# A 3072-point transform on one Trainium2 core: the sequence factored as 64 by 48 in place of 128 by 24

## The chip, the core and the metric

The kernel runs on one core of a Trainium2 chip. A core has TensorE (matrix products, into PSUM), VectorE, ScalarE and GpSimd (in the profile DVE, ACT and POOL), SyncE (SP), whose queue here only issues DMAs, and 16 DMA engines between HBM and SBUF. The metric is the device time of one execution in microseconds; the median of several runs counts.

## What is computed

Eight sequences of 3072 tokens by 256 features go through a spectral layer, then a soft mixture of experts, then a feed-forward layer. The reference, cut to the part that matters here:

```python
X = np.fft.rfft(x, axis=1)                  # x: 8 x 3072 x 256, float32
Xr, Xi = X.real, X.imag
Yr = Xr @ w_r - Xi @ w_i + b_r
Yi = Xr @ w_i + Xi @ w_r + b_i
Yr = np.sign(Yr) * np.maximum(np.abs(Yr) - lam, 0.0)   # lam = 0.01, Yi likewise
y = np.fft.irfft(Yr + 1j * Yi, n=3072, axis=1)
# then over all 24576 tokens of y: soft routing to 8 experts x 4 slots,
# and h = z @ w_in; out = (h * tanh(softplus(h))) @ w_out
```

The change concerns the first line alone, the forward transform, which is written as two stages of matrix products.

## The kernel before

A sequence of 3072 points is factored as 128 x 24: point 24 p + n has p on the 128 partitions and n with the 256 features along the row. **Stage 1** (`stage1`, product on line 193) multiplies by a 128 x 128 table of cosines and sines `f1` over p. A sequence has 6144 columns (24 x 256), taken 512 at a time (`XC`), so there are 12 products for each of 8 sequences, 96 in all, in float32. Each result is copied out of PSUM by ScalarE (line 197; for the first sequence every second one by VectorE, line 195) into a tile `a`. That tile is stored to the DRAM buffer `sdr` (line 200 for the first sequence, `store_a` on line 204 for the others), which turns the layout: `load_b` (line 210) reads it back as 96 rows for each of 32 positions `q`. A position holds two frequencies of the first stage, each with cosine and sine parts of 24 points, so 4 x 24 = 96 rows. **Stage 2** (`stage2`, line 222) multiplies each block of 96 rows by its own 96 x 144 table, a part of `tall`. ScalarE and VectorE split the result into a high and a low half (lines 230 and 231).

After that come, for each quarter `k` of a sequence (32 in all): `linear`, the three products with the weights in split float32 (tiles `l`, line 250), the threshold on VectorE, ScalarE and GpSimd, `project` (`pp`, line 281), `inv1` (`iu`, line 292) and `ytrans` (`tr`, line 307); and for each sequence the routing: `inv2`, the softmax steps, `fwd1` and `fwd2` (`dt`, line 434), `dturn` (`tn`, line 444) and `slots` (`sps`, line 457). `fwd1` and `inv2` use `f1` and its transpose `f1t` too. `pp`, `iu`, `dt` and `sps` and the products of the experts run in tiles of the array: the weights take 32 output columns, and three or four products stand side by side (`tile_position`).

The order is written by hand: every step is put on a list with a position, `at(pos, step, ...)`, the list is sorted, and each engine runs its instructions in that order. A unit of position is one quarter `k`. `s1pos(b, j)` gives the position of product j of sequence b: the loads, products and stores of sequence b + 2 or so run among the quarters of the sequences before. `load_x` and `store_a` handle two products (1024 columns) at a time. PSUM is one pool of 8 banks in rotation. The first sequence runs ahead of everything: twelve loads of x, twelve products, twelve stores, and 36 products that only keep TensorE running (`warm`). The feed-forward layer, the second half of the time, follows when all sequences are done.

Of the kernel before, what the change touches and what calls it, by code (L numbers as in the profile page):

```python
# [17 lines left out]

SEQ, D = 3072, 256
N1, N2 = 128, 24  # L20
NP = 32
NC = 384
NS = 32
# [5 lines left out]

def constants():  # L30

    n1 = np.arange(N1, dtype=np.float64)
    n2 = np.arange(N2, dtype=np.float64)
    f1 = np.zeros((N1, N1))
    t = np.zeros((96, NP, 96))
    w = 2.0 * np.pi / SEQ
    for i in range(64):
        p, par = divmod(i, 2)
        m, r0, c0 = 2 * i, par * 48, par * 24
        q = {0: 1, 1: 0}.get(i, i)  # L40
        if q:
            ang = 2.0 * np.pi * np.mod(n1 * q, N1) / N1
            f1[:, m], f1[:, m + 1] = np.cos(ang), -np.sin(ang)
            for k2 in range(N2):
                a = w * np.mod(n2 * (q + 128 * k2), SEQ)
                sg = 1.0 if k2 < 12 else -1.0
                t[r0:r0 + 24, p, c0 + k2] = np.cos(a)
                t[r0 + 24:r0 + 48, p, c0 + k2] = np.sin(a)
                t[r0:r0 + 24, p, 48 + c0 + k2] = -sg * np.sin(a)
                t[r0 + 24:r0 + 48, p, 48 + c0 + k2] = sg * np.cos(a)  # L50
        else:
            f1[:, m], f1[:, m + 1] = 1.0, np.where(n1 % 2 == 0, 1.0, -1.0)
            for pos in range(23):
                k, r = (128 * (pos + 1), r0) if pos < 11 else (64 + 128 * (pos - 11), r0 + 24)
                a = w * np.mod(n2 * k, SEQ)
                t[r:r + 24, p, c0 + pos] = np.cos(a)
                t[r:r + 24, p, 48 + c0 + pos] = -np.sin(a)
            t[r0:r0 + 24, p, c0 + 23] = 1.0
            t[r0:r0 + 24, p, 48 + c0 + 23] = np.where(n2 % 2 == 0, 1.0, -1.0)
    sel = np.tile(np.eye(NS), (4, 1))  # L60
    big = np.concatenate([f1, f1.T, np.eye(128), sel], axis=1)
    tt = t.transpose(2, 1, 0)
    t3 = np.concatenate([t, t[:, :, 0:48] + t[:, :, 48:96]], axis=2)
    both = np.concatenate([t3.reshape(96, -1), tt.reshape(96, -1)], axis=1)
    return np.ascontiguousarray(big.astype(np.float32)), np.ascontiguousarray(both.astype(np.float32))
# [3 lines left out]
def body(ctx, tc, x, w_r, w_i, b_r, b_i, phi, w1, w2, w_in, w_out, cbig, ct, out, dbg=None, stop=False):  # L69
    nc = tc.nc  # L70
# [31 lines left out]
    def psum(shape, name):  # L102
        return psp.tile(shape, F32, tag="p", name=name)
# [8 lines left out]
    m_run = [const.tile([128, 1], F32, name=f"m_run{i}") for i in range(2)]  # L112
    m_t, ab_t = {}, {}
    wsp = {n: (wp.tile([128, 2, D], F32R, name=n + "h"), wp.tile([128, 2, D], F32R, name=n + "l")) for n in "abc"}
    ph = wp.tile([128, 2, NS], F32, name="ph")
    bias = wp.tile([128, 2, 2], F32, name="bias")
    tlo = wp.tile([128, 2, 2], F32, name="tlo")
# [9 lines left out]

    def setup():
        nc.scalar.preload_act_table_set("natural_log_exp_and_others")
        nc.sync.dma_start(out=cb, in_=cbig)  # L130
        for j in range(na):
            load_x(0, j)
        load_t(0, 0)
        wst = ytp.tile([128, 6, D], F32, tag="yt", name="wst")
        wrf, wif = wst[:, 0:2], wst[:, 2:4]
# [32 lines left out]
        o = NP * 144 * i + g * w  # L168
        nc.sync.dma_start(out=tall[:, o:o + w], in_=ct[:, o:o + w])

    def load_x(b, j):

        w = XC if b == 0 else 2 * XC
        pool, tag = (xp, "x") if b else (yp, "y")
        t = pool.tile([128, w], F32, tag=tag, name="xc")
        src = x[b].rearrange("(p n) d -> p (n d)", p=128)
        nc.sync.dma_start(out=t, in_=src[:, j * w:(j + 1) * w])
        x_t[b, j] = t

    def stage1(b, j):  # L180
        if j == 0:
            sdr[b] = dram.tile([NP, 96, D], F32, tag="sdr", bufs=2, name="sdr")
        if b == 0:
            xs = x_t.pop((b, j))
            a = yp.tile([128, XC], F32, tag="y", name="a")
        else:
            c = slice(j % 2 * XC, j % 2 * XC + XC)
            xs = x_t[b, j // 2][:, c]
            if j % 2 == 0:
                a_t[b, j // 2] = xp.tile([128, 2 * XC], F32, tag="a", name="a")  # L190
            a = a_t[b, j // 2][:, c]
        ps = psum([128, XC], "s1")
        nc.tensor.matmul(ps, lhsT=f1, rhs=xs, start=True, stop=True)  # L193
        if b == 0 and j % 2:
            nc.vector.tensor_copy(a, ps)
        else:
            nc.scalar.activation(out=a, in_=ps, func=AF.Copy)
        if b == 0:
            dst = sdr[b].rearrange("q (r n) d -> (q r) (n d)", r=4)
            nc.sync.dma_start(out=dst[:, j * XC:(j + 1) * XC], in_=a)  # L200

    def store_a(b, i):
        dst = sdr[b].rearrange("q (r n) d -> (q r) (n d)", r=4)
        nc.sync.dma_start(out=dst[:, 2 * i * XC:2 * (i + 1) * XC], in_=a_t.pop((b, i)))
        x_t.pop((b, i))

    def load_b(k):
        b, g = divmod(k, 4)
# [674 lines left out]
```

## Time and profile before

| | |
|---|---|
| median of 3 runs | 1995.38 us (1994.22 to 2002.56) |
| the profiled execution, first to last instruction | 1995.2 us |
| TensorE busy | 1942.3 us, 97% |
| VectorE, ScalarE, GpSimd busy | 1169.1, 903.3 and 195.1 us |
| moved by DMA | 171.39 MB, mean 86 GB/s |
| granted TensorE clock, mean | 0.988 |

The profile is one execution. Its views are: the page, with busy time by engine, the chain of work that ended last, and the costliest groups of instructions; tables of busy time by stretch of time; instructions in order of time, where like ones that follow each other stand in one row with their count; and lists of what an engine waited for. Times are microseconds from the start of the span. TensorE works in a pipeline, so the duration of one matmul covers more than the time for which it keeps others out; the distance from start to start tells that.

### The profile page before, as it was taken

How to read it: one execution, taken by the hardware profiler on the slowest of the kernel's cores; microseconds unless marked ns; L12 is line 12 of the kernel's file. 1: busy time of each engine (PE TensorE's matmuls, PEld its weight loads, DVE VectorE, ACT ScalarE, POOL GpSimd, SP SyncE). 2: the span in 40 equal slices, each digit the busy share in tenths (PEclk: the TensorE clock that was granted, in tenths of full speed). 3: DMA queues.
4: the chain of work that ended last, by engine and by line, in shares of the span. 5: the costliest groups of instructions: out<-in, count | busy, mean ns of one | idle time of the engine just before them, and what ended most of it. 6: DMA issues, size and time to landing. Idle time of an engine off the chain costs nothing.

```text
span 1995.2 us, 30611 instructions
## 1 busy us (share of the span) xinstructions
PE 1942.3 (97%) x12344; PEld 1623.3 (81%) x12344; DVE 1169.1 (59%) x1767; ACT 903.3 (45%) x1479; POOL 195.1 (10%) x245
## 2 busy tenths in 40 slices
PE   7899999999998999999999999999999999999999
PEld 5677787777877768888888888888888888888887
DVE  3345545556455547666666666666666666666665
ACT  2666666667665433333333333333333333333332
POOL 0332332332323100000000000000000000000000
PEclk9999998999999899999999999999999999999999
DMA  8755665566643690002002002002002002000000
GB/s 248 233 151 173 167 185 141 170 173 160 184 142 78 213 297 27 20 13 53 22 22 53 22 22 53 22 22 53 11 22 53 22 22 53 22 22 22 22 22 22
DMA packets 131150, 171.39 MB, mean 86 GB/s; under 512 B 57136, under 2 KB 96688, under 8 KB 130752
## 3 DMA queue, kind: packets, MB, share of 16 engines
q1 hardware_dynamic: 128512, 164.10, 28.0%
q0 software_dynamic: 1792, 4.76, 0.8%
q8 instruction: 97, 1.59, 0.3%
q10 hardware_dynamic: 704, 0.57, 0.1%
q14 instruction: 45, 0.37, 0.1%
HBM read 102.29 MB, written 67.11 MB: 85 GB/s over the span
## 4 chain that ended last, share of the span: by engine, by line
PE 80%; ACT 9%; DVE 6%; issue 2%; POOL 1%; DMA 1%; ACTq 0%; SPq 0%; DVEq 0%; POOLq 0%
PE o L815 54%; PE h L785 9%; PE l L250 5%; DVE xl L231 3%; PE s L222 3%; ACT xh L230 2%; PE s L193 2%; ACT cl L268 2%; ACT p L269 2%; PE sps L457 1%; ACT y L309 1%; PE tr L307 1%; POOL yt L270 1%; DVE p L262 1%; PE pp L281 1%
## 5 line engine op out<-in xcount | busy, mean ns | idle before, releaser
L815 PE MATMUL o<-whl,gh 128*128 128x512 f32 x3072 | 1082.9, 395 | 0.0
L815 PE MATMUL o<-whl,gl 128*128 128x256 f32 x3072 | 827.8, 280 | 0.0
L791 ACT ACTIVATE g<-h 128x1024 f32<-128x1024 f32 x384 | 394.3, 1027 | 746.3 <-PE h L785 733.6
L815 PEld LDWEIGHTS o<-whl,gh 128*128 128x128 f32 x3072 | 566.5, 188 | 121.5
L815 PEld LDWEIGHTS o<-whl,gl 128*128 128x128 f32 x3072 | 578.5, 188 | 31.5
L800 DVE TENSOR_TENSOR gl<-g,gh 128x1024 fp32r<-128x1024 f32 x384 | 470.2, 1224 | 28.9 <-DVE gh L796 0.9
L796 DVE CAST gh<-g 128x1024 fp32r<-128x1024 f32 x384 | 265.8, 692 | 351.1 <-ACT g L791 351.0
L785 PE MATMUL h<-ctt,mst 128*128 128x512 f32 x768 | 240.8, 395 | 0.0
L231 DVE TENSOR_TENSOR xl<-s,xh 128x432 fp32r<-128x432 f32 (+1 forms) x192 | 106.1, 558 | 153.1 <-ACT xh L230 153.1
L270 POOL TENSOR_TENSOR yt<-cl,p 128x384 f32<-128x384 f32 x124 | 126.2, 1017 | 435.1 <-ACT p L269 309.6
L222 PE MATMUL s<-tall,bt 96*128 96x144 f32 x1024 | 137.0, 294 | 8.9 <-DMA bt<-sdr 4.5
L222 PEld LDWEIGHTS s<-tall,bt 96*128 96x128 f32 x1024 | 134.9, 197 | 13.0 <-issue 12.0
L230 ACT ACTIVATE xh<-s 128x432 fp32r<-128x432 f32 (+1 forms) x192 | 90.8, 490 | 114.0 <-DVE xl L231 77.4
L785 PEld LDWEIGHTS h<-ctt,mst 128*128 128x128 f32 x768 | 121.2, 188 | 17.9 <-DVE mst L772 0.5
L262 DVE TENSOR_TENSOR p<-l,k 128x384 f32<-128x384 f32 x128 | 70.6, 553 | 91.3 <-PE l L250 58.9
L823 DVE TENSOR_TENSOR os<-o,os 128x256 f32<-128x256 f32 x192 | 76.6, 419 | 77.4 <-ACT os L822 77.4
L268 ACT ACTIVATE cl<-p,tup 128x384 f32<-128x384 f32 x124 | 76.3, 615 | 91.6 <-DVE p L262 71.4
L193 PE MATMUL s<-xc,cb 128*128 128x512 f32 x192 | 103.8, 632 | 7.8 <-DMA xc<-in_x_dram 7.8
L822 ACT ACTIVATE os<-o 128x256 f32<-128x256 f32 x192 | 73.7, 384 | 41.6 <-PE o L815 37.7
L269 ACT ACTIVATE p<-p,tlo 128x384 f32<-128x384 f32 x124 | 76.4, 616 | 4.0
L309 ACT ACTIVATE y<-tr 96x512 f32<-96x512 f32 x128 | 66.1, 592 | 14.6 <-PE tr L307 14.6
L307 PEld LDWEIGHTS tr<-cb,yt 128*96 128x96 f32 x512 | 54.0, 126 | 18.9 <-DVE xl L231 7.0
(176 smaller groups left out, 1539.7 us busy)
## 6 DMA issues: line engine op xcount, KB each, us to landing
bt<-sdr SPq DMA_DIRECT2D x32, 768.0 KB, 8.2
out_dram<-os SPq DMA_DIRECT2D x47, 512.0 KB, 2.6
xc<-in_x_dram SPq DMA_DIRECT2D x42, 512.0 KB, 5.2
sdr<-a SPq DMA_DIRECT2D x42, 512.0 KB, 3.2
ctt<-c_d SPq DMA_DIRECT2D x28, 384.0 KB, 7.1
c_d<-chl SPq DMA_DIRECT2D x16, 384.0 KB, 3.1
w1t<-in_moe_w_dram SPq DMA_DIRECT2D x6, 1024.0 KB, 6.9
w2t<-in_moe_w_dram SPq DMA_DIRECT2D x5, 1024.0 KB, 11.0
```

What stands on the lines that cost most here:

```text
L193: nc.tensor.matmul(ps, lhsT=f1, rhs=xs, start=True, stop=True)
L222: nc.tensor.matmul(ps[:, i], lhsT=b_t[k][:, p0 + i, h * 128:(h + 1) * 128], rhs=t_m[:, 8 * g + p0 + i, :], start=True, stop=True)
L230: nc.scalar.activation(out=xh, in_=ps, func=AF.Copy)
L231: nc.vector.tensor_sub(part(xl_t[k]), ps, xh.bitcast(F32))
L268: nc.scalar.activation(out=cl, in_=p, func=AF.Relu, bias=tup[:, ri, eh:eh + 1])
L269: nc.scalar.activation(out=p, in_=p, func=AF.Relu, scale=-1.0, bias=tlo[:, ri, eh:eh + 1])
L270: nc.gpsimd.tensor_sub(yt[:, eh, :, ri, :], cl, p)
L785: nc.tensor.matmul(ps[:, i], lhsT=mst[:, f * 128:f * 128 + 128], rhs=ct_t[b][:, 4 * m:4 * m + 4].rearrange("p n t -> p (n t)"), start=True ...
L791: nc.scalar.activation(out=g, in_=h_t.pop(p), func=AF.Mish)
L796: nc.vector.tensor_copy(gh, g)
L800: nc.vector.tensor_sub(gl, g, gh.bitcast(F32))
L815: nc.tensor.matmul(o, lhsT=a[:, i, ts], rhs=w, start=f == 0 and n == 0, stop=f == 15 and n == 1)
```

## The change

The sequence is factored as 64 x 48. Stage 1 multiplies by a 64 x 64 table `f64` over 64 partitions. The other factor, 48 points, is cut in two halves of 24, and each half fills 64 of the 128 partitions: `load_x` loads 64 partitions at a time. A call of `stage1` now takes 1024 columns, as four products of 64 x 64 tables with 512 columns: two halves of partitions (rows of the array) by two halves of columns of x (columns of the array). Each half of rows writes a PSUM bank of its own; the two halves of columns write its partitions 0 to 63 and 64 to 127. There are 48 such calls, and each stands where the second of the two products stood before. Two copies empty the two banks, and the store becomes two DMAs of 64 partitions.

The 32 positions of `sdr` keep their 96 rows, but a position now holds one frequency of the first stage, 2 x 48 rows, and its table in `tall` is the full one for that frequency. Stage 2 and everything behind it keep their shapes. `fwd1` and `inv2` get the table as a 128 x 128 one (`np.kron(f1, np.eye(2))`). For the first sequence the loads of the upper 64 partitions are issued by ScalarE, `f64` is loaded first and `cb` after x, and x and `a` lie in buffers of the pool `bp`.

```diff
+R1, R2 = 64, 48
...
-    f1 = np.zeros((N1, N1))
+    f1 = np.zeros((R1, R1))
...
+    fd = np.kron(f1, np.eye(2))
     sel = np.tile(np.eye(NS), (4, 1))
-    big = np.concatenate([f1, f1.T, np.eye(128), sel], axis=1)
+    big = np.concatenate([fd, fd.T, np.eye(128), sel, np.tile(f1, (2, 1))], axis=1)
...
     def setup():
         nc.scalar.preload_act_table_set("natural_log_exp_and_others")
-        nc.sync.dma_start(out=cb, in_=cbig)
-        for j in range(na):
-            load_x(0, j)
+        nc.sync.dma_start(out=f64, in_=cbig[:, 416:480])
+        for i in range(na // 2):
+            load_x(0, i)
+        nc.sync.dma_start(out=cb, in_=cbig[:, 0:416])
         load_t(0, 0)
...
-    def load_x(b, j):
-
-        w = XC if b == 0 else 2 * XC
-        pool, tag = (xp, "x") if b else (yp, "y")
-        t = pool.tile([128, w], F32, tag=tag, name="xc")
-        src = x[b].rearrange("(p n) d -> p (n d)", p=128)
-        nc.sync.dma_start(out=t, in_=src[:, j * w:(j + 1) * w])
-        x_t[b, j] = t
+    def load_x(b, i):
+        if b:
+            t = xp.tile([128, 2 * XC], F32, tag="x", name="xc")
+        else:
+            if i % 2 == 0:
+                x_t["w"] = bp.tile([128, 2, 2 * XC], F32, tag="xh" if i < 4 else "xl", name="xc")
+            t = x_t["w"][:, i % 2]
+        src = x[b].rearrange("(p h n) d -> h p (n d)", h=2, n=N2)
+        for h in range(2):
+            eng = nc.sync if b or h == 0 else nc.scalar
+            eng.dma_start(out=t[64 * h:64 * h + 64], in_=src[h][:, 2 * i * XC:2 * (i + 1) * XC])
+        x_t[b, i] = t
...
-        ps = psum([128, XC], "s1")
-        nc.tensor.matmul(ps, lhsT=f1, rhs=xs, start=True, stop=True)
-        if b == 0 and j % 2:
-            nc.vector.tensor_copy(a, ps)
-        else:
-            nc.scalar.activation(out=a, in_=ps, func=AF.Copy)
+        ps = [psum([128, XC], "s1") for h in range(2)]
+        for h in range(2):
+            hs = slice(64 * h, 64 * h + 64)
+            for c in range(2):
+                nc.tensor.matmul(ps[h][64 * c:64 * c + 64], lhsT=f64[hs], rhs=t[hs, XC * c:XC * c + XC],
+                                 start=True, stop=True, tile_position=(64 * h, 64 * c))
+        for h in range(2):
+            if b == 0 and h:
+                nc.vector.tensor_copy(a[:, h], ps[h])
+            else:
+                nc.scalar.activation(out=a[:, h], in_=ps[h], func=AF.Copy)
         if b == 0:
...
+            store_a(b, i)

     def store_a(b, i):
-        dst = sdr[b].rearrange("q (r n) d -> (q r) (n d)", r=4)
-        nc.sync.dma_start(out=dst[:, 2 * i * XC:2 * (i + 1) * XC], in_=a_t.pop((b, i)))
-        x_t.pop((b, i))
+        dst = sdr[b].rearrange("q (r h n) d -> (q r) h (n d)", r=2, h=2)
+        a = a_t.pop((b, i))
+        for c in range(2):
+            cols = slice((2 * i + c) * XC, (2 * i + c + 1) * XC)
+            nc.sync.dma_start(out=dst[:, :, cols], in_=a[64 * c:64 * c + 64])
...
-        for j in range(na):
-            at(s1pos(b, j), stage1, b, j)
+        for i in range(na // 2):
+            at(s1pos(b, 2 * i + 1), stage1, b, i)
```

What this does to the order of the instructions, at three places. In the listings a row is an instruction or a run of like ones (x and their number, counted in products, not in passes), with its line, the tile written and the tiles read, and the shape written. `s_` and a number is a PSUM bank, `xc` a tile of x, `f_118` the table `f64`, `cb` the tile with the old table, `tall` the second-stage tables, `dd` and `dtt` tiles of the routing, `xh`, `xl` and `ah` and its like the split operands of `linear`.

TensorE, at the end of the last quarter of a sequence, where the routing's tiled products `dt` and `iu` follow. Before:

```order
L250 MATMUL l<-xl,ch 128x384
L250 MATMUL l<-xh,cl 128x384
L193 MATMUL s_1599<-xc,cb 128x512
L434 MATMUL dt<-tall,dd 32x96 x8
L292 MATMUL iu<-tall,phat 32x96 x8
```

After:

```order
L258 MATMUL l<-xl,ch 128x384
L258 MATMUL l<-xh,cl 128x384
L198 MATMUL s_1643<-xc,f_118 64x512 x2
L198 MATMUL s_1644<-xc,f_118 64x512 x2
L442 MATMUL dt<-tall,dd 32x96 x8
L300 MATMUL iu<-tall,phat 32x96 x8
```

One product of stage 1 has become a group of four, and it stands beside other tiled products.

TensorE, a little later, among the remaining `dt` products and the transposes `tn` that take ScalarE's copies of them. Before:

```order
L444 MATMUL tn<-cb,dtt 96x128 x2
L434 MATMUL dt<-tall,dd 32x96 x8
L193 MATMUL s_1712<-xc,cb 128x512
L444 MATMUL tn<-cb,dtt 96x128 x2
L250 MATMUL l<-xh,ch 128x384
```

After:

```order
L452 MATMUL tn<-cb,dtt 96x128 x2
L442 MATMUL dt<-tall,dd 32x96 x8
L452 MATMUL tn<-cb,dtt 96x128 x2
L258 MATMUL l<-xh,ch 128x384
L258 MATMUL l<-xl,ch 128x384
```

The product of stage 1 between `dt` and `tn` is gone; its columns are in the next group, some twenty rows on.

SP, at the start. Before:

```order
L130 DMA cb<-in_cbig_dram 128x416
L177 DMA xc<-in_x_dram 128x512 x12
L169 DMA tall<-in_ct_dram 96x1152
L200 DMA sdr<-a 128x512 x12
L210 DMA bt<-sdr 96x8x256
```

After:

```order
L128 DMA f_118<-in_cbig_dram 128x64
L180 DMA xc<-in_x_dram 64x1024 x6
L131 DMA cb<-in_cbig_dram 128x416
L168 DMA tall<-in_ct_dram 96x1152
L213 DMA sdr<-a 128x1x512 x12
L218 DMA bt<-sdr 96x8x256
```

Six of the twelve loads of x have left SP; ScalarE issues them behind its table load.

## Rows read from the trace of the kernel before

**Rows 1.** The page: busy time and instructions by engine, the chain, line L193.

```profile
PE 1942.3 (97%) x12344; PEld 1623.3 (81%) x12344; DVE 1169.1 (59%) x1767; ACT 903.3 (45%) x1479; POOL 195.1 (10%) x245
...
PE 80%; ACT 9%; DVE 6%; issue 2%; POOL 1%; DMA 1%; ACTq 0%; SPq 0%; DVEq 0%; POOLq 0%
...
L193 PE MATMUL s<-xc,cb 128*128 128x512 f32 x192 | 103.8, 632 | 7.8 <-DMA xc<-in_x_dram 7.8
```

**Rows 2.** Busy time by stretch: length, each engine, TensorE clock, DMA share, GB/s.

```profile
35.00:110.00 75.00, 67.27 (x410) 56.04 (x409) 31.28 (x71) 44.63 (x90) 17.75 (x22) 0.94 0.71 204
110.00:565.00 455.00, 438.15 (x3455) 348.68 (x3453) 247.57 (x530) 305.12 (x633) 143.28 (x179) 0.99 0.59 165
...
735.00:1995.20 1260.20, 1255.90 (x6921) 1083.70 (x6920) 798.80 (x967) 468.31 (x583) 0.00 (x0) 1.00 0.10 31
```

**Rows 3.** TensorE in order of time near 274 us: start, duration, line, tiles, shape.

```profile
274.30 0.34 PE L250 MATMUL l<-xh,bl 128*128 128x384 f32 x1
274.48 1.02 PE L193 MATMUL s<-xc,cb 128*128 128x512 f32 x2
...
275.51 0.34 PE L250 MATMUL l<-xl,ch 128*128 128x384 f32 x1
```

**Rows 4.** TensorE in order of time near 287 us, around a tiled group.

```profile
287.07 0.34 PE L250 MATMUL l<-xh,cl 128*128 128x384 f32 x1
287.33 0.54 PE L292 MATMUL iu<-tall,phat 96*32 96x96 f32 x16
287.80 1.12 PE L193 MATMUL s<-xc,cb 128*128 128x512 f32 x2
...
288.94 0.34 PE L250 MATMUL l<-xl,ah 128*128 128x386 f32 x1
```

**Rows 5.** TensorE in order of time near 720 us, the experts' first layer.

```profile
719.77 1.92 PE L697 MATMUL hp<-w1t,sit 128*32 128x512 f32 x16
721.51 0.83 PE L713 MATMUL so<-w2t,ht 128*32 128x256 f32 x12
```

**Rows 6.** TensorE in order of time near 726 us, the experts' second layer.

```profile
726.51 0.40 PE L713 MATMUL so<-w2t,ht 128*32 128x256 f32 x1 [0.34 <-DVE ht L707]
726.52 0.42 PE L713 MATMUL so<-raw,ht 128*32 128x256 f32 x3
726.75 0.38 PE L713 MATMUL so<-w2t,ht 128*32 128x256 f32 x1
```

**Rows 7.** Line L193 alone, 110 to 565 us: count, durations, first and last start.

```profile
L193 PE MATMUL s<-xc,cb x138: 590/592/1222, 110.0 to 560.7; 128*128 128x512 f32 x138
```

**Rows 8.** What TensorE waited for, 35 to 110 us: total, times, longest.

```profile
PE s L222 <- DMA bt<-sdr: 4.5, 1, 4.5
PE s L193 <- DMA xc<-in_x_dram: 1.9, 2, 1.7
```

**Rows 9.** What TensorE waited for, 110 to 565 us.

```profile
PE tn L444 <- ACT dtt L437: 4.9, 5, 1.5
```

**Rows 10.** All engines in order of time, the start; SPq is the SP queue.

```profile
1.18 9.54 SPq L177 DMA_DIRECT2D xc<-in_x_dram  x12
...
6.19 0.60 ACT L197 ACTIVATE a<-s 128x512 f32<-128x512 f32 x1 [4.17 <-PE s L193]
...
12.48 9.19 SPq L200 DMA_DIRECT2D sdr<-a  x12
...
26.09 0.34 SPq L210 DMA_DIRECT2D bt<-sdr  x1
```

**Rows 11.** Busy time by stretch, the start.

```profile
2.00:11.00 9.00, 5.03 (x6) 1.89 (x7) 0.69 (x1) 0.62 (x2) 3.02 (x5) 1.00 0.87 247
11.00:25.00 14.00, 14.00 (x60) 8.50 (x60) 6.97 (x12) 2.99 (x5) 0.00 (x0) 1.00 1.02 371
```

**Rows 12.** Groups by line: the eviction of a first-stage product on ScalarE.

```profile
L197 ACT ACTIVATE a<-s 128x512 f32<-128x512 f32 x90 | 52.9, 588 | 16.0 <-PE s L193 16.0
```

**Rows 13.** What the SP queue waited for, 0 to 700 us: the stores of stage 1.

```profile
SPq L204 <- ACT a L197: 120.3, 20, 12.4
```

More of the change, by code (lines that the diff above doesn't have):

```diff
@@ L30, in constants @@
 def constants():
-    n1 = np.arange(N1, dtype=np.float64)
-    n2 = np.arange(N2, dtype=np.float64)
-    f1 = np.zeros((N1, N1))
+    n1 = np.arange(R1, dtype=np.float64)
+    n2 = np.arange(R2, dtype=np.float64)
+    f1 = np.zeros((R1, R1))
     t = np.zeros((96, NP, 96))
     w = 2.0 * np.pi / SEQ
[L37 to L50, printed above, removed]
-        else:
[L52 to L59, printed above, removed]
@@ new lines, in constants @@
+    f1[:, 0], f1[:, 1] = 1.0, np.where(n1 % 2 == 0, 1.0, -1.0)
+    for pos in range(47):
+        k, r = (R1 * (pos + 1), 0) if pos < 23 else (R1 // 2 + R1 * (pos - 23), R2)
+        a = w * np.mod(n2 * k, SEQ)
+        t[r:r + R2, 0, pos] = np.cos(a)
+        t[r:r + R2, 0, 48 + pos] = -np.sin(a)
+    t[0:R2, 0, 47] = 1.0
+    t[0:R2, 0, 95] = np.where(n2 % 2 == 0, 1.0, -1.0)
+    for q in range(1, NP):
+        ang = 2.0 * np.pi * np.mod(n1 * q, R1) / R1
+        f1[:, 2 * q], f1[:, 2 * q + 1] = np.cos(ang), -np.sin(ang)
+        for k2 in range(R2):
+            a = w * np.mod(n2 * (q + R1 * k2), SEQ)
+            sg = 1.0 if k2 < R2 // 2 else -1.0
+            t[0:R2, q, k2] = np.cos(a)
+            t[R2:96, q, k2] = np.sin(a)
+            t[0:R2, q, 48 + k2] = -sg * np.sin(a)
+            t[R2:96, q, 48 + k2] = sg * np.cos(a)
@@ L114, in body @@
     wsp = {n: (wp.tile([128, 2, D], F32R, name=n + "h"), wp.tile([128, 2, D], F32R, name=n + "l")) for n in "abc"}
+    f64 = wp.tile([128, R1], F32, name="f64")
     ph = wp.tile([128, 2, NS], F32, name="ph")
@@ L169, in load_t @@
         nc.sync.dma_start(out=tall[:, o:o + w], in_=ct[:, o:o + w])
-    def load_x(b, j):
-        w = XC if b == 0 else 2 * XC
-        pool, tag = (xp, "x") if b else (yp, "y")
-        t = pool.tile([128, w], F32, tag=tag, name="xc")
-        src = x[b].rearrange("(p n) d -> p (n d)", p=128)
-        nc.sync.dma_start(out=t, in_=src[:, j * w:(j + 1) * w])
-        x_t[b, j] = t
-    def stage1(b, j):
-        if j == 0:
-            sdr[b] = dram.tile([NP, 96, D], F32, tag="sdr", bufs=2, name="sdr")
-        if b == 0:
[L184 to L191, printed above, removed]
-        ps = psum([128, XC], "s1")
-        nc.tensor.matmul(ps, lhsT=f1, rhs=xs, start=True, stop=True)
-        if b == 0 and j % 2:
-            nc.vector.tensor_copy(a, ps)
-        else:
-            nc.scalar.activation(out=a, in_=ps, func=AF.Copy)
-        if b == 0:
-            dst = sdr[b].rearrange("q (r n) d -> (q r) (n d)", r=4)
-            nc.sync.dma_start(out=dst[:, j * XC:(j + 1) * XC], in_=a)
@@ L202, in store_a @@
-    def store_a(b, i):
-        dst = sdr[b].rearrange("q (r n) d -> (q r) (n d)", r=4)
-        nc.sync.dma_start(out=dst[:, 2 * i * XC:2 * (i + 1) * XC], in_=a_t.pop((b, i)))
-        x_t.pop((b, i))
+    def load_x(b, i):
[10 more added lines that the diff above has]
+        x_t[b, i] = t
@@ new lines, in stage1 @@
+    def stage1(b, i):
+        if i == 0:
+            sdr[b] = dram.tile([NP, 96, D], F32, tag="sdr", bufs=2, name="sdr")
+        t = x_t.pop((b, i))
+        if b or i > 3:
+            a = xp.tile([128, 2, XC], F32, tag="a", name="a")
+        else:
+            if i % 2 == 0:
+                a_t["w"] = bp.tile([128, 2, 2, XC], F32, tag="b", name="a")
+            a = a_t["w"][:, i % 2]
+        a_t[b, i] = a
+        ps = [psum([128, XC], "s1") for h in range(2)]
[7 more added lines that the diff above has]
+                nc.vector.tensor_copy(a[:, h], ps[h])
+            else:
+                nc.scalar.activation(out=a[:, h], in_=ps[h], func=AF.Copy)
+        if b == 0:
+            store_a(b, i)
```

## The prediction

> **What bounds the kernel now.** I read the page first, for the engines' shares and the chain that ended last, then a table of busy time by stretch, and then single stretches of TensorE in order of time. TensorE is busy 97% of the span and makes up 80% of the chain, and the line that the change rewrites, L193, has 192 matmul instructions [rows 1]. The table of stretches says where a gain can land. From 735 us on, the feed-forward half (1260 us of the span) has TensorE busy throughout and nothing in the change touches it. From 110 to 565 us, where most of the first-stage products stand, TensorE is busy 438 of 455 us at a granted clock of 0.99 (the 2.4 GHz level), VectorE 248, ScalarE 305 and the DMA engines 59% [rows 2]. So time taken off TensorE there should come off the span, with ScalarE the next to fill. Between 35 and 110 us it is less clear: TensorE is busy 67 of 75 us and the DMA engines 71% [rows 2].
>
> **What a first-stage product costs.** A product of 128x512 in float32 stands in the trace as two instructions. Around 274.5 us it sits between two second-layer products (`l`): the product starts at 274.48 and the second `l` after it at 275.51, which is 1.03 us; one `l` takes 0.18 (274.30 to 274.48), so the product holds TensorE for 0.85 us, 0.425 for each of its two passes [rows 3]. The duration printed beside an instruction contains its pipeline and is not used. The change puts two products (one load of x, 1024 columns) into one group of four 64x64 pieces of 512 columns each, so a pair costs 2 x 0.85 = 1.70 us before. There are 192 / 4 = 48 pairs; 12 of the 96 products, 6 pairs, belong to the start, and 42 pairs lie in the loop. 138 instructions lie between 110 and 565 us [rows 7], which is 34.5 pairs, and the other 7.5 pairs lie before.
>
> **What a group of four costs.** It is 8 instructions of one pass each. No row tiling stands in the trace of before, but column tiling does. In the experts' first layer 16 instructions, each with 512 columns and a tile of 32 output columns, start at 719.77 and the next work at 721.51: 1.74 us, where one after the other they would take 16 x 0.425 = 6.8. Four ran at a time, at 0.435 for each set of four [rows 5]. So two column pieces certainly overlap. Whether the two row halves do as well is the open term. If they do, 8 instructions take 2 sets, 0.85 us. If not, they take 4 sets, 1.70 us, which is what the pair costs now. I take 2 sets, because the row that comes nearest is one where pieces of the array work side by side at no loss, four streams at a time, and four streams is what is asked here.
>
> That needs the first passes of all four pieces ahead of the second passes. The expert rows show it for columns: pieces that differ in the name of their weight tile start as one and three, and then the one again, its second pass, 0.24 us later, so the first pass of each product starts ahead of the second pass of its neighbour [rows 6]. The Trainium skill (TensorE: Matmul & The Clock Gate, section Part 3, "What overlaps and what doesn't") says otherwise: matmuls keep strict order in start and end, with no reordering. By that rule a product's second pass would hold back the neighbour's first, and these rows speak against it. What it would give here is the last rival below.
>
> **The price of changing the shape of the array.** The kernel changes it already, for `iu` among others. From 287.07 (an `l`) to 288.94 (the second `l` after) is 1.87 us; inside lie one `l` (0.18), `iu` in four sets of 96 columns (4 x 0.425 x 96/512 = 0.32), one product (0.85) and another `l` (0.18), together 1.53. The rest, 0.34 us, is what it costs to go into the tiled shape and back [rows 4], 0.17 for each of the two changes. The group therefore holds TensorE for 0.85 + 0.34 = 1.19 us against 1.70: 0.51 us less for each pair.
>
> **Where it lands.** Between 110 and 565 us: 34.5 x 0.51 = 17.6 us. Before 110 us: 7.5 x 0.51 = 3.8, of which I count half, 1.9, since TensorE waits there for loads of `bt` (4.5 us) and of x (1.9 us), which it would meet sooner [rows 8]. In the order of the instructions about every second group stands beside work that is tiled already (`dt`, `iu` or `pp`). Three changes of shape then do for two tiled pieces that had needed four: 21 x 0.15 = 3.1 us (bounds 0 and 21 x 0.17 = 3.6).
>
> **What it costs elsewhere.** The evictions stay as many, 0.59 us each on ScalarE [rows 12], but two of them now come at once, and single products no longer stand as filler between work and the eviction that it waits for. The second piece of order shows one such filler gone, between `dt` and `tn`, where TensorE has already waited for ScalarE's eviction in five places, 4.9 us in all [rows 9]. If every one of the 42 groups lost the second eviction, that were 42 x 0.59 = 24.8 us; if none, nothing, since 8 PSUM buffers rotate. I take 0.1 us for each group, 4.2 us, near the lower end, as the waits in [rows 9] are 5 us in a stretch of 455. On the SP queue x and `sdr` become two DMAs each. SP stands waiting for the evicted tile 120 us in all [rows 13], so 84 more issues of some 0.4 us (the twelve loads of x at the start took 0.8 each on the mean [rows 10]) hide in that wait. Queued behind them are loads of `bt` and the stores of `udr`; if this cover is gone, the price is one issue for each load, under 1 us in places that have slack. Stores write runs of 2 KB in place of 4 KB, as the stores at the start do already; I put that at nothing with the DMA engines at 59%. VectorE, the second-stage products, the inverse transform and the tables keep their shapes: nothing.
>
> **The start.** SP issues twelve loads of x ahead of everything, and so the first store of stage 1 is issued at 12.48 us although its eviction ran at 6.19 [rows 10]. In the changed order SP issues six and ScalarE six, so stores can go out earlier. The DMA engines are 87% busy from 2 to 11 us at 247 GB/s, and full from 11 to 25 us at 371 GB/s [rows 11]. That is 7.4 MB, which at 371 GB/s throughout would take 20 us in place of 23: at most 3.0 us gained, and at worst one more issue ahead of x (0.4 us) lost. I take 1.0 us gained, since the engines are near full. TensorE's shorter first stage hides behind these transfers.
>
> **The sum.** 17.6 + 1.9 + 3.1 - 4.2 + 1.0 = 19.4 us less. The profiled span is 1995.2 us and the median of the runs 1995.38, so the two agree and the sum goes from 1995.4: **1976 us**. With every bound at its best it is 21.4 + 3.6 + 3.0 = 28 less, 1967 us.
>
> **Rivals.** All take the pair's price in the loop, 42 times.
> 1. *Rows don't overlap* (slower). Four sets: 1.70 + 0.34 = 2.04 us, 0.34 more than now; 42 x 0.34 = 14.3, less 1.0 at the start: about 2009 us. It decides as soon as a group needs more than (1.70 - 0.34) / 0.425 = 3.2 sets. For it: no row shows row tiling, and both halves write the same PSUM partitions at once. Against it: the halves write different banks, and read different SBUF partitions, which the overlapping column pieces don't even do.
> 2. *Rows overlap, but the second pass of a piece goes ahead of the first pass of the piece below it.* Three sets: 1.275 + 0.34 = 1.615, 0.085 less than now, 3.6 in all and 1.0 at the start: about 1991 us. [Rows 6] speak against it, for columns alone.
> 3. *TensorE is faster, but evictions take it back.* At half the bound above, 12.4 instead of 4.2, and nothing for shared changes of shape: 17.6 + 1.9 + 1.0 - 12.4 = 8.1 less, 1987 us. ScalarE busy 305 of 455 us speaks against it, its bursts for it. The Trainium skill (TensorEngine Tiling (Array Packing), section PSUM Bottleneck) warns of just this: tiling speeds the matmul and not the eviction, which may become the limit.
> 4. *Strict order, as the rule above has it.* Five sets: 2.13 + 0.34 = 2.47, 0.77 more than now, 42 x 0.77 = 32: about 2027 us.
>
> **How the numbers follow.** Forecast 0.60; rival 1 0.15; rival 2 0.12; rival 3 0.08; rival 4 0.05. A difference of 0.5%, 10 us, is about what a measurement of this kernel can tell from no change. Faster by more than that needs a time under 1985.4: the forecast less a twentieth of it, 0.57. Within: that twentieth (0.03), rivals 2 and 3, 0.23. Slower: rivals 1 and 4, 0.20. The range reaches from the best bound, 1967, over the forecast and rivals 3 and 2 (0.80 together), with 5 us for the latter's costs: 1967 to 1996.
>
> **What would show it.** In the loop the time from the start of a group to the `l` behind it tells the number of sets: about 1.2 us for two, 1.6 for three, 2.0 for four. The line should have 384 instructions. Right is also: TensorE's waits for ScalarE between 110 and 565 us grow by a few us only, and `bt` is first issued a us or so before 26.09 [rows 10]. I am wrong if the group takes 1.6 us or more, or if it takes 1.2 and the stretch up to the end of the first stage is not some 20 us shorter; then `bt`, `tn` or `l` should show new waits for DMA or ScalarE.

## The result, and the profile after

The changed kernel took **2009.09 us** (median of four runs, 2006.32 to 2010.61) where the kernel before took 1995.74 in the same comparison: a ratio of 1.0062, 95% interval 1.0043 to 1.0080. It was forecast 19.4 us faster and is some 12 us slower. The profiled execution has a span of 2004.5 us.

The page answers to [rows 1]; the last line is that of the first-stage products.

```profile
PE 1920.4 (96%) x12536; PEld 1593.4 (79%) x12536; DVE 1167.5 (58%) x1767; ACT 902.1 (45%) x1479; POOL 194.5 (10%) x245
...
PE 79%; ACT 7%; DVE 6%; DMA 4%; issue 2%; POOL 2%; SPq 1%; ACTq 0%; DVEq 0%; POOLq 0%
...
L198 PE MATMUL s<-xc,f 64*64 64x512 f32 x384 | 62.2, 690 | 12.4 <-DMA xc<-in_x_dram 10.7
```

TensorE works 22 us less than before (1920.4 against 1942.3), so the change did what it was made to do. But the span is 9 us longer, and DMA, 1% of the chain before, is 4% now. Busy time by stretch, to be read beside [rows 2, 11]:

```profile
2.00:11.00 9.00, 3.12 (x16) 0.64 (x16) 0.69 (x1) 0.62 (x2) 3.03 (x5) 1.00 1.02 244
11.00:25.00 14.00, 11.87 (x80) 6.29 (x77) 7.43 (x13) 2.99 (x5) 0.00 (x0) 1.00 1.05 317
35.00:110.00 75.00, 62.01 (x417) 49.91 (x420) 30.15 (x68) 41.14 (x83) 16.77 (x21) 0.90 0.88 215
110.00:565.00 455.00, 421.48 (x3560) 325.50 (x3555) 240.05 (x520) 299.94 (x625) 139.28 (x173) 0.97 0.66 164
744.00:2004.50 1260.50, 1256.04 (x6921) 1083.71 (x6920) 798.83 (x968) 468.35 (x583) 0.00 (x0) 1.00 0.10 31
```

The feed-forward half takes what it took (1260 us) and starts 9 us later, so what was lost was lost before it. From 110 to 565 us TensorE now stands idle 33.5 us where it stood 17, and the granted clock fell from 0.99 to 0.97. What it waited for there (engine, line, product, releaser: total, times, longest), to be read beside [rows 9]:

```profile
PE lps L330 <- DMA v<-udr: 13.3, 4, 4.6
PE tn L452 <- ACT dtt L445: 8.2, 5, 2.0
PE s L230 <- ACT dm L409: 3.1, 5, 0.7
PE tr L315 <- DVE xl L239: 2.4, 5, 0.5
PE lps L330 <- DVE xl L239: 2.2, 1, 2.2
```

`v` is the routing's input (`c_load`), read back from the scratch that `udr` stores fill; TensorE did not wait for it in this stretch before. Of the other names here and below, `lps` is the product of `inv2` with `v` and `lg` ScalarE's copy of it; `rm` and `mt` are the softmax's maximum on VectorE and its transpose; `dm` is ScalarE's copy of the product `dps` of `fwd1`; `xl` is the low half of the second stage's result. All waits of this stretch sum to 33.1 us against 16.6. Those for ScalarE alone are 14.0 against 9.9, 4.1 more, so what grew most is the wait for one DMA. The clock comes on top. These are five of the six stretches in which it was granted at half (columns as in the table above, the clock third from the end):

```profile
222.50:230.00 7.50, 6.11 (x34) 2.51 (x35) 4.31 (x8) 5.24 (x12) 0.28 (x1) 0.77 0.64 142
305.00:310.00 5.00, 4.71 (x21) 1.56 (x24) 2.16 (x5) 2.90 (x7) 0.00 (x0) 0.66 0.74 150
337.50:345.00 7.50, 7.33 (x54) 5.94 (x55) 0.99 (x3) 3.41 (x10) 2.98 (x5) 0.56 0.86 208
390.00:397.50 7.50, 6.17 (x34) 2.60 (x35) 4.36 (x9) 4.25 (x9) 0.00 (x0) 0.77 0.35 69
...
472.50:482.50 10.00, 7.45 (x36) 3.30 (x37) 5.62 (x11) 5.84 (x13) 0.85 (x2) 0.66 0.58 124
```

A mean of 0.77 over 7.5 us is 3.45 us at the lower level (1.2 GHz) and the rest at 2.4 GHz. The one left out is 425 to 430 us, at 0.66. Four of the six lie right at the end of a wait for `v` (2.6 to 4.6 us), the other two, from about 338 and 426 us, at or shortly behind the end of a wait of `tn` for `dtt` of 1.9 and 2.0 us. Length times missing share of the clock, summed over the six, is 13.6 us of full-rate time. The profile of before has two such stretches between the same times:

```profile
307.50:315.00 7.50, 7.13 (x35) 5.30 (x35) 5.04 (x13) 4.19 (x8) 2.29 (x3) 0.55 0.43 131
332.50:340.00 7.50, 6.05 (x50) 4.44 (x51) 1.77 (x4) 4.68 (x14) 3.19 (x4) 0.77 0.90 262
```

One stands among three waits of 0.9, 0.8 and 0.4 us within 3 us, the other behind a `tn` wait of 1.5, and they are worth 5.1 us. So waits (+16.5) and clock (+8.5) together take back 25 us in a stretch where TensorE was to give 20.7. A fixed stretch does not hold the same work, though. From the first `lps` of the first sequence to that of the sixth (138.9 to 545.8 us before, 141.0 to 556.7 after) the time grew from 406.9 to 415.7 us: 17 us more of waits and 8.5 of clock, so TensorE gave about 17 us for these 30 groups, and the stretch lost 9.

Why `v` is late stands in the SP queue, in order of time. After, and then before:

```profile
462.57 1.76 SPq L308 DMA_DIRECT2D udr<-u  x4
465.10 1.20 SPq L213 DMA_DIRECT2D sdr<-a  x2
466.40 1.68 SPq L180 DMA_DIRECT2D xc<-in_x_dram  x2
468.25 0.90 SPq L322 DMA_DIRECT2D v<-udr  x1
```

```profile
454.97 1.77 SPq L300 DMA_DIRECT2D udr<-u  x4
457.00 0.34 SPq L204 DMA_DIRECT2D sdr<-a  x1
457.44 0.38 SPq L177 DMA_DIRECT2D xc<-in_x_dram  x1
457.99 0.64 SPq L314 DMA_DIRECT2D v<-udr  x1
```

`v` waits for its turn behind a store and a load of the first stage. These two issues took 0.72 us, the four that replace them take 2.88, and `v` is issued 5.7 us after the first `udr` store instead of 3.0. It then needs 6.7 us to land. Before, it needed 6.1, landed near 464.1 and was used at 465.2: about 1 us of slack.

### The profile page after: what moved, and what is told of

It is laid out like the page before. It is cut to its first block, busy times and chain, and to the rows that moved or that the text cites. A ratio compares the mean times of both kernels' runs of the same rounds, so it can differ in the third digit from the quotient of the medians.

```text
span 2004.5 us, 31115 instructions
## 1 busy us (share of the span) xinstructions
PE 1920.4 (96%) x12536; PEld 1593.4 (79%) x12536; DVE 1167.5 (58%) x1767; ACT 902.1 (45%) x1479; POOL 194.5 (10%) x245
## 4 chain that ended last, share of the span: by engine, by line
PE 79%; ACT 7%; DVE 6%; DMA 4%; issue 2%; POOL 2%; SPq 1%; ACTq 0%; DVEq 0%; POOLq 0%
PE o L823 54%; PE h L793 9%; PE l L258 5%; DVE xl L239 3%; PE s L230 2%; ACT xh L238 2%; DMA v<-udr 1%; ACT cl L276 1%; DMA xc<-in_x_dram 1%; PE tr L315 1%; PE sps L465 1%; PE s L198 1%; POOL yt L278 1%; ACT p L277 1%; DVE p L270 1%
## 5 line engine op out<-in xcount | busy, mean ns | idle before, releaser
L230 PE MATMUL s<-tall,bt 96*128 96x144 f32 x1024 | 138.3, 293 | 19.4 <-DMA bt<-sdr 8.3
L198 PE MATMUL s<-xc,f 64*64 64x512 f32 x384 | 62.2, 690 | 12.4 <-DMA xc<-in_x_dram 10.7
L315 PE MATMUL tr<-cb,yt 128*96 128x128 f32 x512 | 66.5, 276 | 4.3 <-DVE xl L239 3.2
## 6 DMA issues: line engine op xcount, KB each, us to landing
w2t<-in_moe_w_dram SPq DMA_DIRECT2D x5, 1024.0 KB, 11.8
```

Source lines behind the costliest of these rows:

```text
L230: nc.tensor.matmul(ps[:, i], lhsT=b_t[k][:, p0 + i, h * 128:(h + 1) * 128], rhs=t_m[:, 8 * g + p0 + i, :], start=True, stop=True)
```

## Experiments

The theories, as the expectations name them. **Q**: stage 1's doubled DMAs delay the `v` load on SP. **E**: evictions in pairs, and filler lost between a product and the eviction it waits for. **P**: transfers of 64 partitions are slower. **S**: the start. **F**: ScalarE and VectorE end last wherever the groups stand. Kernels measured together share a chip and the runs of the kernel before, so between such batches the ratios are compared, and within one the medians. The ratio takes in every run, so it can differ by a us or so from that of the medians.

### The v load moved forward

```diff
-PA = dict(... cl=0.78 ...)
+PA = dict(... cl=0.4815 ...)    # v right behind the udr stores
```

> The changed kernel, with one step moved on the SP queue: the load of v (c_load) is issued right behind the udr stores it needs, ahead of two sdr stores and two x loads. Theory Q (the doubled DMAs of stage 1 stand ahead of the v load on SP, and TensorE's lps waits for it): lps waits for v fall from 13.3 us to under 3, about 4 us come off each of 6 sequences, 1983 to 1990 us. Theory E (evictions in pairs and lost filler hold TensorE up): no change, 2006 to 2011 us.

Measured 2003.41 us, ratio 1.0047 (1.0030 to 1.0063). The waits for `v` are gone, but others came up behind them. Waits from 110 to 565 us:

```profile
PE tn L452 <- ACT dtt L445: 8.1, 5, 2.0
PE tr L315 <- ACT lg L331: 4.6, 5, 1.1
```

By the time alone the gain (0.15%) isn't certain; in its trace the first product of the feed-forward half starts at 740.0 instead of 744.1 us. Q is real and far too small: 13 us of waits removed brought about 4. Nor is it the turn on the queue alone. Near 460 us this kernel still issues `v` 3.7 us after the first `udr` store, later than the 3.0 of the kernel before, but ahead of the stage-1 DMAs it lands in 3.2 us (median of six) instead of 5.6.

### Doubled DMAs without the change

```diff
 # kernel before: x loads and sdr stores, from the second sequence on, as two DMAs each
+e3: 64 partitions each, runs of 4 KB      e5: 128 partitions, half the columns, runs of 2 KB
```

> The kernel before, TensorE as it was, but the loads of x and the stores of sdr after the first sequence are two DMAs of 64 partitions each, runs of 4 KB as before. Theory Q: part of the loss shows here without any change on TensorE, 1998 to 2005 us, with the v load issued 1 to 3 us later behind its udr stores than in the kernel before (3.0 us). Theory E: within 3 us of the kernel before. Theory P (a DMA of 64 partitions moves its packets slower): slower here than with two DMAs of 128 partitions, and longer times to landing.

> The kernel before, with the same doubling of DMAs after the first sequence, but each over 128 partitions and half the columns (runs of 2 KB). Theory Q: as slow as the split by partitions, 1998 to 2005 us. Theory P: nearer to the kernel before, 1994 to 1998 us. Theory E: within 3 us of the kernel before.

Measured in one batch: 1998.40 us for the 64-partition pairs (ratio 1.0015, 0.9999 to 1.0030), 1991.59 for the half columns (0.9991, 0.9978 to 1.0003). The number of DMAs costs nothing that these runs can tell; between the two shapes lie 0.24%, some 5 us. From the page, KB of one DMA and median us from issue to landing, first of the 64-partition kernel, then of the half columns:

```profile
xc<-in_x_dram SPq DMA_DIRECT2D x96, 256.0 KB, 4.9
sdr<-a SPq DMA_DIRECT2D x96, 256.0 KB, 3.6
```

```profile
xc<-in_x_dram SPq DMA_DIRECT2D x96, 256.0 KB, 3.9
sdr<-a SPq DMA_DIRECT2D x96, 256.0 KB, 3.4
```

The kernel before, undivided, moves 128 partitions in the same runs of 4 KB:

```profile
xc<-in_x_dram SPq DMA_DIRECT2D x42, 512.0 KB, 5.2
```

So 64 partitions take nearly as long for half the bytes, and the length of the runs isn't why. They take longer to issue too: the medians are 0.56 us for a store and 0.65 for a load of x with 64 partitions, 0.38 and 0.44 with 128. P holds. Four waits for `v` (8.7 us) appeared in the 64-partition kernel, which has none of the change but these DMAs; with the half columns, as many DMAs, it is one of 1.3 us. So most of Q is P: two more issues ahead of `v` matter because they are of 64 partitions.

### The second eviction on VectorE

```diff
-            if b == 0 and h:
+            if h:
                 nc.vector.tensor_copy(a[:, h], ps[h])
```

> The changed kernel, with the second of the two evictions of each group on VectorE in place of ScalarE, all sequences. Theory E: ScalarE's bursts are halved, tn waits fall from 8.2 us to about 4, 10 us or more come off, 1995 to 2000 us. Theory Q: the v load still comes late, 2004 to 2011 us.

Measured 2000.17 us, 1.0033 (1.0020 to 1.0045): 0.3%, some 6 us, under the changed kernel, with `v` still waited for (11.8 us) and `tn` 5.7 instead of 8.2. Half of the evictions are still ScalarE's, so E probably costs more than the 4.2 us of the forecast; with the interval of this one step alone that isn't certain.

### One group moved, the start undone, pairs in the kernel before, three mends

```diff
 # e6: the first group of a sequence between the second dt and the first tn
-            at(s1pos(b, 2 * i + 1), stage1, b, i)
+            at(4 * b - 5.395 if b > 2 and i == 0 else s1pos(b, 2 * i + 1), stage1, b, i)
 # e7: the first sequence in whole products, with cb[:, 0:128] (the 128 x 128 kron table) and 128-partition DMAs
 # e8, kernel before: products in pairs where the groups stand
-            at(s1pos(b, j), stage1, b, j)
+            at(s1pos(b, j | 1) if b else s1pos(b, j), stage1, b, j)
 # e9: e6, e7 and the v load moved forward, together
```

> The changed kernel with one thing moved: from the fourth sequence on, the first group of each sequence stands between the second set of dt products and the first tn transposes instead of ahead of the first dt, so that TensorE has 1.2 us of work while ScalarE evicts dt, and the group's two evictions are queued behind that eviction instead of ahead of it. Theory E now reads: the waits of tn for dtt (8.2 us in five places, up to 2.0 us) are each followed some 2 us later by a stretch of 4 us at half the clock (340 to 344 and 426 to 430 us), so the place costs its wait and about 2 us more: with the filler back tn waits 3 us at most in sum, the half-clock stretches behind the tn places go, and the time is 2000 to 2004 (5 to 9 us less). If only the wait counts and the clock falls for another reason: 2004 to 2006. Theory Q or P (DMAs alone): unchanged, 2007 to 2010.

> The changed kernel, with the first sequence's first stage as in the kernel before (128 x 128 table made from the new factors, whole-width loads and stores of 128 partitions on SP, one product of 512 columns at a time); the sequences after it in groups of four. Theory S (the start lost 2.6 us because 64-partition loads of 4 KB packets land slower and the tables stand behind them): the first second-stage product comes at 33 us or earlier again and the time is 2006 to 2007 (2.5 to 3 less). If the start's loss is made up by slack later: 2009, same. If the first sequence's form also held up what follows (loads of the second sequence, wait for bt at 105 us): 2002 to 2005.

> The kernel before with one thing changed: from the second sequence on, the first stage's products (whole 128 x 128 array, loads and stores as before) stand in pairs back to back at the positions that the groups have in the changed kernel. TensorE work, DMAs and tables are those of before. Theory E (pairs of evictions, lost filler between dt and tn, and the clock that falls behind the longer wait): 1998 to 2003, tn waits for dtt over 8 us, half-clock stretches behind them. If the order costs nothing by itself: 1993 to 1995.

> The changed kernel with three mends at once: the v load right behind the udr stores, the first group between dt and tn, and the first sequence's first stage in whole products. If the three causes (v late behind doubled issues, filler lost, start slower) are what turned the forecast over and they add: 2009 - 6 - 7 - 3 = 1993, with no lps wait for v, tn waits under 3 us, and half-clock stretches only where the kernel before has them; if each of them also frees the clock, 1985 to 1990. If the first stage's gain is lost elsewhere (slower 64-partition transfers in every wait): 1998 or more.

Measured: e6 1.0058 (1.0033 to 1.0083), which the time can't tell from the changed kernel, though `tn` waits 2.9 us instead of 8.2 and no half-clock stretch stands behind a `tn` any more; e7 1.0050 (1.0031 to 1.0070), by its time not certainly faster either, the first second-stage product at 31.6 us instead of 35.7; e8 1.0025 (1.0011 to 1.0038), which is 3.8 us more than the kernel before by the medians and 5 by the ratio; e9 **1991.34 us**, 0.9993 (0.9979 to 1.0008). The waits of e8, from 110 to 565 us, and then two of the kernel before:

```profile
PE tn L444 <- ACT dtt L437: 5.2, 5, 1.5
PE tr L307 <- ACT lg L323: 3.6, 5, 1.1
PE s L222 <- ACT dm L401: 2.4, 4, 0.6
```

```profile
PE mt L338 <- DVE rm L333: 4.6, 6, 0.8
PE l L250 <- ACT lg L323: 3.6, 6, 0.9
```

The waits of `tr` for `lg` and of `s` for `dm`, seen above in the changed kernels, stand here without groups, narrow DMAs or new tables, so they come with the places of the pairs. By the order of the program the reason would be this: a pair right behind `lps` or `dps` takes two of the eight rotating PSUM buffers and two evictions at once, just where `lg` or `dm` is awaited. They are not all new, though. The kernel before waited as long for `lg`, with `l`, and longer for `rm`; all waits of e8 sum to 19.0 us against 16.6, and its clock is full where the kernel before lost 5.1 us. So this one trace doesn't show where e8's 4 to 5 us are lost. The three mends bring the kernel level with the one before and end its half-clock stretches between 110 and 565 us, but not to 1976.

### Other places

```diff
-            at(s1pos(b, 2 * i + 1), stage1, b, i)
+            at(s1pos(b, 2 * i + (b < 3)), stage1, b, i)      # e10; e11 with v and the start as in e9
 # e12: e11 with the second sequence in whole products and 128-partition DMAs too
 # e13: the kernel before, its products in pairs at these places
```

> The changed kernel with one thing moved: from the fourth sequence on, each group stands at the place where the first product of its pair stood in the kernel before, instead of the second's; then none stands right behind lps or dps or ahead of the first dt, and one stands between the third tn and the fourth dt. Theory E (the place of the groups: two evictions on ScalarE and two PSUM banks just where lg, dm and dtt are waited for) expects tn for dtt under 5 us, no waits of tr for lg and s for dm, the half-clock stretches behind the tn places gone, 2001 to 2004; the waits of lps for v (12 us) stay. Theory P (slower 64-partition transfers everywhere) expects 2007 to 2010. If these places are worse: xc waited for, 2010 or more.

> The changed kernel with the v load right behind the udr stores, the first sequence's first stage in whole products, and from the fourth sequence on the groups at the places of the first of each pair. If the places were what held back the rest of the gain in the kernel with three mends (1991; its gain of about 3.7 us a sequence in s, l and dt was lost again in waits of tr for lg, s for dm, tr for xl and a later lps): 1981 to 1987. If the gain is lost to any place, since ScalarE and VectorE are then what ends last: 1990 to 1993.

> The kernel of the run above with the second sequence's first stage in whole products and whole-width loads and stores too. Theory P (64-partition transfers are slower, and the second sequence's stores and bt load are waited for by TensorE for 8 us near 95 us where the kernel before waits 4.5): bt is waited for 5 us or less there, and the time is 3 to 4 us under the run above. If the wait for bt comes from something else: no difference.

> The kernel before with its first-stage products, from the second sequence on, in pairs back to back at the places that the groups have in the two runs above. The control for the places: if pairs cost nothing there, 1993 to 1995 (the pairs at the other places: 3.8 us more); if any pairing costs, 1996 to 1999. What the runs above are below this one is then the worth of the four-tile products together with the narrower transfers.

Measured: e10 **1994.51 us**, 1.0006 (0.9992 to 1.0019); e11 1993.72, 1.0008; e12 1993.83, 0.9998 (0.9985 to 1.0011); e13 2002.09, 1.0042 (1.0019 to 1.0065). Moving the groups is the largest single step, 0.56%, more than `v`, the start or the evictions on VectorE. But with `v` and the start mended as well nothing is added. One line each of the waits of e10 and e11 (110 to 565 us), and one stretch of e11:

```profile
PE lps L330 <- DMA v<-udr: 10.1, 5, 3.8
```

```profile
PE mt L366 <- DVE rm L361: 11.6, 5, 2.4
```

```profile
387.50:395.00 7.50, 7.50 (x26) 5.21 (x26) 5.22 (x7) 4.68 (x9) 1.80 (x3) 0.54 0.21 49
```

With `v` early and no group left between `lps` and `mt`, TensorE waits for the softmax's maximum on VectorE, up to 2.4 us a sequence, and behind four of these five waits the clock is at half for a while, as it was behind the others. It is the places again: e13, the kernel before with its products there, has the same wait, 11.4 us. In e10, where `v` is late, it is 5.3; that the late `v` had hidden the rest is argued. The whole second sequence shortens the wait for `bt` near 95 us from 8.4 to 7.4 us only and does nothing for the time: P is not what holds that place.

### Chosen places

```diff
-            at(s1pos(b, 2 * i + 1), stage1, b, i)
+            at(4 * b - 4 + (-1.395, -1.21, -0.53, 0.15, 1.335, 1.512)[i] if b > 2
+               else s1pos(b, 2 * i + 1), stage1, b, i)      # e14, with v and the start as in e9
 # e15: the kernel before, its products in pairs at these places (v as before)
 # e16: e14, the second eviction of groups 0, 1 and 4 on VectorE
```

> The changed kernel with the v load right behind the udr stores, the first sequence's first stage in whole products, and from the fourth sequence on each group at a place chosen from the waits of the runs before: two behind the second and the fourth dt (in front of the tn that waits for their eviction), one just ahead of mt (which waited 2.4 us each time for rm when the group stood ahead of lps), one behind mb, none right behind lps or dps. Theory E (the places decide whether the gain of about 3.7 us a sequence in s, l and dt reaches the end) expects tn and mt waits of 3 us or less each in sum, no half-clock stretch between 110 and 565 us but one or two, and 1982 to 1988. Theory F (ScalarE and VectorE end last there in any case, and the gain turns into waits wherever the groups stand): 1990 to 1994, with new waits of some other product in the place of those removed.

> The control: the kernel before with its first-stage products from the fourth sequence on in pairs at the same places as the groups of the run above (whole products, loads, stores and the v load as before). If pairs of whole products cost as at the other two sets of places: 1997 to 2002; if these places are good ones: 1992 to 1995. The run above less this one is what the four-tile groups are worth at like places: 8 to 12 us by theory E, 3 to 5 us if the narrower transfers take most of it.

> The kernel with the chosen places, and the second eviction of the groups beside dt, tn and mt (three of six in a sequence) on VectorE instead of ScalarE. Theory E: what ScalarE still delays there (dtt, lg) comes 0.5 us sooner, 1 to 4 us under the run with the chosen places. If VectorE is the engine that rm and mt wait for: the same or 1 to 3 us more.

Measured: e14 **1986.87 us**, ratio **0.9978** (0.9966 to 0.9990), faster than both kernels, though only by 0.2% than the one before; e15 1995.60, 1.0014 (1.0001 to 1.0026); e16 1991.20, 0.9995 (0.9984 to 1.0006). Waits of e14 from 110 to 565 us, its three largest, and the stretch itself, of e14 and then e15:

```profile
PE tr L335 <- DVE xl L259: 3.0, 6, 0.9
PE dt L462 <- DMA dd<-ddr: 2.9, 5, 1.4
PE mt L366 <- DVE rm L361: 2.8, 5, 0.6
```

```profile
110.00:565.00 455.00, 431.05 (x3700) 335.18 (x3698) 252.32 (x547) 309.99 (x649) 145.03 (x180) 1.00 0.68 170
```

```profile
110.00:565.00 455.00, 440.04 (x3463) 346.78 (x3462) 248.32 (x531) 303.49 (x633) 140.33 (x177) 1.00 0.60 166
```

No wait is over 1.4 us and the clock is full throughout. At like places the four-tile kernel is 8.7 us faster than whole products (8.4 at the places of e11 and e13; by the ratios about 7 each), with `v` moved forward in the first of each two. That is E against F: a good part of the gain can reach the end, if the groups stand where something waits anyway. It is about half of the 17.6 us forecast for the loop; e14 still waits 22.7 us in this stretch, e15 13.6. Where the other half goes the same work tells, from the first `lps` of the first sequence to that of the sixth, again e14 and then e15:

```profile
139.40:534.20 394.80, 374.74 (x3254) 292.01 (x3254) 219.22 (x475) 267.99 (x562) 124.94 (x154) 1.00 0.69 174
```

```profile
137.10:541.60 404.50, 390.88 (x3135) 307.39 (x3134) 221.05 (x475) 269.38 (x564) 123.99 (x156) 1.00 0.60 168
```

At full clock in both, TensorE works 16.1 us less for 30 groups, 0.54 each; the forecast was 0.51, and 0.58 with the shared changes of shape. Of these, 6.4 us turn into waits and 9.7 reach the end of the stretch. Evictions on VectorE (e16) make it 4.3 us worse. That VectorE, which `rm` and `xl` need, is then the late one isn't shown: `mt` waits for `rm` 2.8 us as in e14, the waits of `tr` for `xl` grow by 0.4, and new are 1.6 us of `l` for `dm`.

## Why the prediction was wrong

**The group on TensorE: right.** The time from a group to the `l` behind it is the test that the prediction named. TensorE in order of time:

```profile
265.64 0.34 PE L258 MATMUL l<-xh,al 128*128 128x384 f32 x1
265.91 1.09 PE L198 MATMUL s<-xc,f 64*64 64x512 f32 x8
266.93 0.44 PE L258 MATMUL l<-xh,bh 128*128 128x384 f32 x1
267.20 0.34 PE L258 MATMUL l<-xl,bh 128*128 128x384 f32 x1
```

From the `l` at 265.64 to the second `l` behind the group, 267.20, are 1.56 us; less two `l` at 0.18 that is **1.20 us** a group, forecast 1.19, and the line has 384 instructions. Two sets, rows and columns side by side, with the price of changing the shape in it. The pair of e14 and e15 says the same of the whole loop, 0.54 us a group. Rivals 1, 2 and 4 (four, three, five sets) are out: the trace has all four first passes at 265.907 to 265.927 and the second passes 0.48 us later. In which order the program holds these passes the trace doesn't tell, so the five sets that rival 4 drew from the strict order are out, and whether the rule itself holds stays open.

**The evictions and the lost filler: the term mis-sized, the largest step by the runs.** 4.2 us were counted, 0.1 for a group, by the waits that were there. In the changed kernel's own trace the waits for ScalarE grew by 4.1 us, so the sign that the prediction named came true; with `v` out of the way (e1) they are 8.9 more, and moving the groups alone, with all that hangs on their places, is worth 0.56%, 11 us. Pairs of whole products cost the kernel before 3.8, 9.1 and 4.2 us at three sets of places (by the ratios 5.0, 8.4 and 2.8), where the term had no price for the place at all. Rival 3 (evictions take it back, 0.08) was near that size with 12.4 us, and lacked `v`, the start and the clock.

**The SP queue: the step that failed outright.** "84 more issues of some 0.4 us hide in that wait" added SP's idle time up over the whole span [rows 13], but what counts is the order inside the queue. Of the loads behind those issues it named `bt` and not `v`, which had about 1 us of slack. And an issue takes 0.55 to 1.0 us there, not 0.4: in the kernel with half columns, where an issue does take about 0.4, the 84 cost `v` only 1.3 us of waits. `v` came to 13.3 us of waits, the largest growth in the trace.

**64 partitions at nothing: wrong.** The sentence looked at the length of the runs and not at the partitions. The 64-partition DMAs alone, without the change, cost some 5 us against the half columns and made `v` late. The Trainium skill speaks against such a split (SBUF — State Buffer, sections "Door 1: The DMA port swizzle" and "Can I just issue two DMAs to hit both halves?"): partitions 0 to 63 reach 8 of the 16 ports, with 196 GB/s measured at 1 MiB against 328 for all 128 partitions, and two DMAs to the two halves do not make up for it. The runs agree in direction, 4.9 us against 3.9 for 256 KB; that ports are the cause no run here shows.

**The start: wrong sign.** 1.0 us gained was forecast, and `bt` issued before 26.09.

```profile
1.19 9.12 SPq L180 DMA_DIRECT2D xc<-in_x_dram  x6
...
13.10 0.33 SPq L131 DMA_DIRECT2D cb<-in_cbig_dram  x1
...
15.11 10.32 SPq L213 DMA_DIRECT2D sdr<-a  x12
...
29.34 0.34 SPq L218 DMA_DIRECT2D bt<-sdr  x1
```

Six loads on SP take as long as twelve did [rows 10], the tables now queue behind them, and the first store goes out at 15.11 instead of 12.48. The DMA engines are busier at less: 317 GB/s from 11 to 25 us against 371 [rows 11]. `bt` is issued 3.2 us later, and undoing the start (e7) brought the first second-stage product back by 4 us. At the first `lps`, 141.0 against 138.9 us, the changed kernel is still 2.1 us behind, so the 1.9 us counted before 110 us didn't show either.

**The clock: in no term.** Each wait of about 2 us or more that the change made was counted, where at all, at its own length. Six half-clock stretches, 13.6 us against 5.1, came with them. That the mends add up so unevenly because the first ones remove a wait and leave the next, with its slow stretch behind it, is argued; e11, where `mt` waits in place of `lps`, has 13.6 us again.

What stays open: whether other places would bring back the 6.4 us that e14 loses to small waits; why e8 is slower than its trace shows; and the longer wait for `bt` near 95 us, which no changed kernel removed. One DMA of 128 partitions for both halves of x, which would keep the wide transfer, wasn't tried.

## What to carry to other kernels

A faster block of work is also two results at once: before counting its gain, list for each place that it stands at what is evicted, loaded or reduced next, and who waits for that. For a DMA that is added to a queue, look up what is queued behind it and how much slack that has, instead of the queue's idle time; and measure whether its shape makes it slower, since halving a DMA by partitions isn't halving it by columns. If a change is right on its engine and wrong in total time, move the work before giving it up: here the same groups at other places, with `v` early and the first sequence in whole products, went from 2009 to 1987 us.

## What the runs showed of the hardware

- Four float32 products of 64x64 tiles with 512 columns each, two passes apiece, run as two sets: 1.20 us with the changes of shape (0.34) included, 1.70 for the same work in whole products.
- 256 KB into 64 partitions landed in 4.9 us, the same into 128 partitions in 3.9, and 512 KB into 128 partitions in 5.2 (medians). The issue on SP took 0.65 us with 64 partitions and 0.44 with 128.
- Single waits of 1.9 to 2.4 us (`tn` for `dtt`, `mt` for `rm`) were followed by 3.4 to 6.9 us at half the granted clock (the means above, 0.66 over 5 us and 0.54 over 7.5), though not every such wait was. With all waits at 1.4 us or less (e14, 110 to 565 us) the clock stayed at 1.00; but the kernel before fell to half among waits of 0.9, 0.8 and 0.4 us, so the length of a single wait doesn't decide it.
